# A two-dimensional Fourier filter with a gated layer: the first stage issued in one written order, and matmul banks kept in two sets

## The chip, the core and the metric

One Trainium2 chip, one core. The metric is the device time of one execution of the kernel in microseconds (us). The engines run their own instruction streams in order and wait for one another by semaphores: TensorE (PE, with its weight loads PEld), VectorE (DVE), ScalarE (ACT), GpSimd (POOL) and SyncE (SP, which here only issues DMAs). PE writes to PSUM, which has eight banks of 512 float32 columns in each of 128 partitions; DVE and ACT read it from there.

## The reference

```python
S, D, F = 2048, 640, 1728
def A(x, w_r, w_i):                       # spectral filter
    X = rfft2(x, axes=(S, D)) * (w_r + 1j * w_i)      # S x 321
    return irfft2(X, s=(S, D))
def B(x, w_gate, w_up, w_down):           # bilinear gated layer
    return ((x @ w_gate) * (x @ w_up)) @ w_down
h  = x + A(layernorm(x), w_r, w_i)
h2 = h + B(layernorm(h), w_gate, w_up, w_down)
```

Everything is float32. Where precision is to be had from the faster matmul format, operands are split into a high part in that format (fp32r) and the remainder ("lo").

## The kernel before, in words

The 2048 rows are cut into 16 tiles of 128 rows (tile t holds rows t, t+16, ...), the 321 frequencies of the row direction into parts of at most 161. Transforms are matmuls with tables.

1. **First stage** (lines 118 to 296), a loop over the 16 tiles. Each tile needs the mean and the inverse root of the variance of its rows. For 7 tiles DVE takes them (`bn_stats` L134 and L135, `bn_aggr` L136), for 9 tiles ACT does with two passes that add up (L149, L150); tiles are treated in groups of 1, 1, 2, 2, 4, 4 and 2, and each group ends in a square root on ACT (L159) and four small DVE instructions (L160 to L163). Then the row is folded onto itself: `odd` (L183, the differences, on GpSimd), `even` (L193, the sums, on DVE), and from these the 66 columns L197 and the 320 columns L198, both on DVE. The 128 x 128 table `cct` is scaled by the inverse root (L217 on DVE, L215 on ACT for tile 0). PE multiplies the folds by that table: seven products for a tile (L209, L210), each in two instructions, in two PSUM banks `im` and `re`. ACT copies them to the array `s1` with two instructions (L223, 128 columns; L228, 512 columns). Fold buffers are a ring of `NR = 4`, scaled tables a ring of four, PSUM buffers a ring of two. What the loop calls when sets the order on each engine; work on the statistics of later groups is dealt out over the tiles by `spread` and `zipped`.
2. **Filter stage**, a loop over 16 groups of columns g: `d_mm(g)` (transform of rows, banks `re`, `im`), `d_out` (ACT, L330 to L333), `s2_mm` (second transform, into one of two two-bank buffers `u` and `v` handed out by `twin`), `filt` (DVE multiplies by the complex weights, L354 to L357), `is2_mm` (inverse second transform, L389 to L398), `is2_out` (ACT and DVE copy it to `qm` and, split in high and low part, to `qr`; GpSimd corrects one row, L421 and L422). The tables of a group come by `load_wm` and `load_wi` on the SP queue, each with a ring of three. The last groups (lines 462 to 483) are written out one by one.
3. **Inverse transform of rows**, a loop over the 16 tiles: `id_mm(t)` needs all of `qm` and `qr` for the tile, `unfold` (ACT L519, DVE L523 to L525, GpSimd L527) unfolds it, `is1_mm` and `acc` add the result to x.
4. **Gated layer**, from about 175 us to the end, with weights split and combined on the way.

The order of all instructions is the order in which the program issues them (`manual_schedule`); waits follow from the data and from buffers that are used again. PSUM is handed out in pools: until the filter stage ends, one pool "a" holds `re`, `im` (two buffers each), `u` and `v`. It is closed at line 645, and the inverse transform opens "py" (`y`, two pairs of banks) and "pthree" (`eo`, two pairs). A tile of a new pool waits for what last used those banks.

Of the kernel before, what the change touches and what calls it, by code (L numbers as in the profile page):

```python
# [24 lines left out]
NR = 4  # L25
ON_ACT = (1, 4, 10, 14)
EPS = 1e-5
# [19 lines left out]
def tile_spectral_glu(ctx: ExitStack, tc: tile.TileContext, x, wf, wgu, wlast, wdown, wdlast,  # L47
# [12 lines left out]
    def banks(key, name):  # L60
        if key in pools:
            open_pools[key].close()
        open_pools[key] = ExitStack()
        pools[key] = open_pools[key].enter_context(tc.tile_pool(name=name, bufs=2, space=bass.MemoryType.PSUM))

    def bank(tag, bufs=2):
        return pools["a"].tile([P, 512], F32, tag=tag, name=tag, bufs=bufs)

    def pair(tag):
        return pools["a" if tag == "eo" else "y"].tile([P, 2, 512], F32, tag=tag, name=tag, bufs=2)  # L70
# [41 lines left out]
    fold = home("qm", [P, NR * 1026 + 2 * D], "fold")  # L112
# [3 lines left out]
    crs, edge = ([cut(bits, 1536 + 512 * h + P * i, P) for i in range(4)] for h in range(2))  # L116
# [7 lines left out]
    def moments(ts, junk=None, total=None):  # L124
        n = len(ts)
        m2 = small.tile([P, n], F32, tag="m2", name="m2")
        ve = small.tile([P, n], F32, tag="ve", name="ve")
        if junk is None:
            mv = small.tile([P, n, 2], F32, tag="mv", name="mv")

            def one(t, i):
                st = small.tile([P, 2, 6], F32, tag="st", name="st")
                return [
                    lambda: nc.vector.bn_stats(st[:, 0], X[t][:, 0:320]),  # L134
                    lambda: nc.vector.bn_stats(st[:, 1], X[t][:, 320:640]),  # L135
                    lambda: nc.vector.bn_aggr(mv[:, i], st),  # L136
                ]
# [5 lines left out]
        sq = small.tile([P, n], F32, tag="sq", name="sq")  # L143
# [11 lines left out]
    def inverse_root(ve, r, n):  # L155
        sd = small.tile([P, n], F32, tag="sd", name="sd")
        w = small.tile([P, n], F32, tag="w", name="w")
# [8 lines left out]
    SC = {}  # L166

    def front(ts):
        n = len(ts)
        r = small.tile([P, n], F32, tag="r", name="r")  # L170
        junk = [fold[:, o:o + D] for o in (NR * 1026, NR * 1026 + D)]
        m2, ve, fs = moments(ts, junk * 2 if ts[0] in ON_ACT else None)
        for i, t in enumerate(ts):
            SC[t] = r[:, i:i + 1], m2[:, i:i + 1]
        return fs, inverse_root(ve, r, n)

    def folded(t):
        o = t % NR * 1026
        return fold[:, o:o + 642], fold[:, o + 642:o + 1026]

    def odd(t):
        f = folded(t)[0]
        nc.gpsimd.tensor_tensor(view(f, 0, [[160, 2], [1, 160]]), view(XP[t], 1, [[320, 2], [1, 160]]),  # L183
                                view(XP[t], 639, [[-320, 2], [-1, 160]]), op=OP.subtract)

    def even(t):
        f, j = folded(t)

        def both(n):
            return view(f, 0, [[320, 2], [1, n]]), view(f, 160, [[321, 2], [1, n]])  # L190

        return [
            lambda: nc.vector.scalar_tensor_tensor(view(f, 320, [[161, 2], [1, 161]]),  # L193
                                                   view(XP[t], 0, [[320, 2], [1, 161]]), SC[t][1],
                                                   view(XP[t], 640, [[-320, 2], [-1, 161]]),
                                                   op0=OP.subtract, op1=OP.add),
            lambda: tt(view(j, 33, [[-33, 2], [1, 33]]), *both(33), op=OP.add),  # L197
            lambda: tt(view(j, 64, [[1, 2], [2, 160]]), *both(160), op=OP.subtract),  # L198
        ]

    PS1, CR = {}, {}

    def s1_mm(t):
        pm, pr = PS1[t] = bank("im"), bank("re")
        (f, j), c = folded(t), CR[t]
        sums = [(f[:, o:o + P], f[:, o + n:o + n + P]) for o, n in ((31, 160), (353, 161))]
        for k, ls in enumerate((*sums, (view(j, 128, [[2, P]]),), (view(j, 129, [[2, P]]),))):
            for n, l in enumerate(ls):
                nc.tensor.matmul(pm[:, k * P:(k + 1) * P], l, c, start=n == 0, stop=n == len(ls) - 1)  # L209
        nc.tensor.matmul(pr[:, 0:P], j[:, 0:P], c, start=True, stop=True)  # L210

    def scale_c(t):
        CR[t] = crs[t % 4]
        if t == 0:
            act(CR[t], cct, AF.Copy, scale=SC[t][0])  # L215
        else:
            nc.vector.tensor_scalar(CR[t], cct, SC[t][0], None, op0=OP.mult)  # L217

    def at(base, t):
        return view(base, 4 * t, [[64, 32], [1, 4]])  # L220

    def s1_rest(t):
        act(at(s1[:, 4], t), PS1[t][1][:, 0:P].rearrange("p (g m) -> p g m", g=32), AF.Copy)  # L223

    def s1_main(t):
        n = 4 if t < NT - 1 else 2
        for c in range(0, 4, n):
            act(view(s1, 4 * t + 2048 * c, [[2048, n], [64, 32], [1, 4]]),  # L228
                PS1[t][0][:, c * P:(c + n) * P].rearrange("p (c g m) -> p c g m", c=n, g=32), AF.Copy)
# [5 lines left out]
    banks("a", "pone")  # L235
    dve = [[] for _ in range(NT)]
# [1099 lines left out]
```

## Time and profile before

| | |
|---|---|
| median of 3 runs | 703.7 us (703.69 to 704.72) |
| the profiled execution | 704.37 us, its span 702.6 us |
| PE busy | 686.4 us (98%) |
| weight loads | 605.2 us (86%) |
| DVE | 478.9 us (68%) |
| GpSimd | 375.6 us (53%) |
| ACT | 305.0 us (43%) |
| DMA | 60.30 MB, mean 86 GB/s |

A row of a timeline gives the start in us from the beginning of the span, the length in us, the engine, the line, the operation, the tile written and the tiles read, their shapes, how many instructions are merged in the row, and in brackets how long the engine had stood idle before it and what released it. A row of a group gives the count, the total busy time in us and the mean of one in ns. A row of a stage gives the busy time of each engine with its instruction count and then the granted PE clock as a share of full speed. Durations overlap a little on DVE and ACT (an instruction starts before the last has quite ended), so costs in a full stream are read from one start to the next.

### The profile page before, as it was taken

What the parts mean: (1) busy time and instruction counts of PE and PEld (TensorE: products, weight loads), DVE (VectorE), ACT (ScalarE), POOL (GpSimd) and SP (SyncE); (2) the same over time, 40 slices, a digit from 0 to 9 for tenths busy, and PEclk for the clock granted to TensorE, in tenths of its full rate; (3) what the DMA queues carried; (4) which work ended last, traced back from release to release, by engine and by line L of the source; (5) the groups of instructions that cost most, each with busy time, mean ns of one, the idle gap of its engine ahead of it and who ended that gap; (6) DMA issues with size and microseconds to landing.
All of it is one profiled execution on the core that took longest, in us unless ns stands there. A gap on an engine that the chain in (4) does not pass through costs nothing.

```text
span 702.6 us, 10125 instructions
## 1 busy us (share of the span) xinstructions
PE 686.4 (98%) x3784; PEld 605.2 (86%) x3784; DVE 478.9 (68%) x832; ACT 305.0 (43%) x584; POOL 375.6 (53%) x355
## 2 busy tenths in 40 slices
PE   7899998999999999999999999999999999999998
PEld 7789997987888898988888889888888988888887
DVE  7968887699888445656565658664666656565654
ACT  4866776356543323242523356252333342424320
POOL 3312225332154586877868643158596977868610
PEclk9999999999999999999999999999999999999999
DMA  9406764002321211203020263311211102030203
GB/s 335 185 6 204 227 210 166 1 0 94 132 76 38 75 39 37 76 1 113 0 86 28 94 219 118 113 38 37 76 38 58 55 11 102 0 107 7 75 1 150
DMA packets 23233, 60.30 MB, mean 86 GB/s; under 512 B 2576, under 2 KB 7184, under 8 KB 23184
## 3 DMA queue, kind: packets, MB, share of 16 engines
q1 hardware_dynamic: 22608, 57.94, 24.0%
q0 software_dynamic: 288, 1.48, 0.6%
q8 instruction: 30, 0.49, 0.3%
q10 hardware_dynamic: 288, 0.23, 0.1%
q14 instruction: 19, 0.16, 0.1%
HBM read 51.78 MB, written 7.86 MB: 85 GB/s over the span
## 4 chain that ended last, share of the span: by engine, by line
PE 87%; DVE 8%; ACT 3%; issue 2%; DMA 1%; DVEq 0%
PE e L82 47%; PE y L82 26%; PE re L82 2%; PE im L82 2%; PE eo L82 2%; PE v L342 1%; PE im L209 1%; DVE ex L777 1%; PE u L342 1%; PE e L570 1%; DVE x L540 1%; ACT fold L149 1%; DMA x<-in_x_dram 1%; ACT fold L150 1%; DVE q L523 1%
## 5 line engine op out<-in xcount | busy, mean ns | idle before, releaser
L82 PE MATMUL e<-xt,wst 128*128 128x512 f32 x864 | 219.1, 391 | 0.0
L82 PEld LDWEIGHTS e<-xt,wst 128*128 128x128 f32 x864 | 157.9, 188 | 27.3 <-DVE m L1037 0.3
L82 PE MATMUL y<-wd,ht 128*128 128x320 f32 x880 | 150.6, 309 | 0.1
L82 PEld LDWEIGHTS y<-wd,ht 128*128 128x128 f32 x880 | 138.9, 188 | 11.3 <-DVE xb L538 0.6
L741 POOL TENSOR_TENSOR wst<-raw,wst 128x1024 fp32r<-128x1024 f32 x24 | 59.6, 2485 | 90.7 <-ACT wst L740 78.4
L82 PE MATMUL e<-t,wst 128*128 128x512 f32 x288 | 74.2, 391 | 0.0
L757 POOL TENSOR_TENSOR wst<-raw,wst 128x896 fp32r<-128x896 f32 (+1 forms) x46 | 65.1, 1438 | 7.8 <-ACT wst L752 7.8
L952 DVE TENSOR_TENSOR xb<-y,xb 128x640 f32<-128x640 f32 x60 | 49.4, 824 | 26.4 <-PE y L82 24.5
L773 ACT ACTIVATE ht<-e 128x512 fp32r<-128x512 f32 x48 | 27.6, 596 | 86.1 <-DVE rawh L870 44.2
L82 PEld LDWEIGHTS e<-t,wst 128*128 128x128 f32 x288 | 52.6, 188 | 8.6
L952 DVE TENSOR_TENSOR x<-y,x 128x640 f32<-128x640 f32 x48 | 39.5, 823 | 21.1 <-PE y L82 19.6
L1037 DVE TENSOR_TENSOR m<-e,m 128x512 f32<-128x512 f32 x24 | 16.5, 687 | 46.1 <-ACT m L1030 28.6
L777 DVE TENSOR_TENSOR ht<-e,ht 128x512 fp32r<-128x512 f32 x48 | 33.0, 688 | 16.8 <-ACT ht L773 16.3
L752 ACT ACTIVATE wst<-raw 128x896 fp32r<-128x896 f32 (+1 forms) x48 | 30.1, 677 | 31.1 <-POOL raw L746 30.4
L82 PE MATMUL y<-ex,ht 128*128 128x320 f32 x216 | 43.5, 310 | 0.0
L82 PE MATMUL e<-xt,wdir 128*128 128x512 f32 x180 | 42.1, 392 | 0.0
L494 POOL TENSOR_TENSOR wd<-draw,wd 128x640 fp32r<-128x640 f32 x10 | 15.6, 1576 | 46.2 <-ACT wd L493 46.2
L82 PEld LDWEIGHTS e<-xt,wdir 128*128 128x128 f32 x180 | 33.5, 188 | 7.2 <-issue 0.2
L82 PEld LDWEIGHTS y<-ex,ht 128*128 128x128 f32 x216 | 36.3, 188 | 3.1
L908 ACT ACTIVATE wd<-draw 128x640 fp32r<-128x640 f32 x18 | 13.3, 740 | 58.7 <-POOL draw L921 48.1
L82 PE MATMUL e<-ht,wst 128*128 128x512 f32 x144 | 38.4, 392 | 0.0
L538 DVE TENSOR_TENSOR x<-y,x 128x640 f32<-128x640 f32 x32 | 26.2, 819 | 15.9 <-PE y L82 15.9
(228 smaller groups left out, 1300.5 us busy)
## 6 DMA issues: line engine op xcount, KB each, us to landing
raw<-in_wgu_dram SPq DMA_DIRECT2D x24, 640.0 KB, 4.0
wts<-in_wf_dram SPq DMA_DIRECT2D x16, 644.0 KB, 4.4
draw<-in_wdown_dram SPq DMA_DIRECT2D x24, 320.0 KB, 4.5
x<-in_x_dram SPq DMA_DIRECT2D x16, 320.5 KB, 6.1
bits<-in_mm_dram SPq DMA_DIRECT2D x32, 128.0 KB, 4.0
sp<-x SPq DMA_DIRECT2D x8, 320.0 KB, 2.2
xb<-sp SPq DMA_DIRECT2D x8, 320.0 KB, 6.1
out_dram<-x SPq DMA_DIRECT2D x8, 320.0 KB, 2.2
```

What stands on the lines that cost most here:

```text
L82: nc.tensor.matmul(o, l, r, start=start, stop=stop, skip_group_check=True)
L342: nc.tensor.matmul(ps[h][:, 0:NQ], WM[g][0][:, h], T[g][:, h], start=True, stop=True)
L494: los.append(lambda r=r, a=a, b=b: engine.tensor_tensor(w[:, 1, a:b], r, f32(w[:, 0, a:b]), op=OP.subtract))
L538: tt(xv, ps[:, :, 0:320], xv, op=OP.add)
L741: nc.gpsimd.tensor_tensor(wa[:, 1], stage[:, 0:1024], f32(wa[:, 0]), op=OP.subtract)
L752: act(ws[:, 0, o:o + b - a], stage[:, a:b], AF.Copy)
L757: ptt(ws[:, 1, o:o + b - a], stage[:, a:b], f32(ws[:, 0, o:o + b - a]), op=OP.subtract)
L773: act(unit(u)[0], src, AF.Copy)
L777: engine.tensor_tensor(lo, src, f32(hi), op=OP.subtract)
L908: act(w[:, 0, a:b], r, AF.Copy)
L952: tt(xv, PQ[q][:, :, 0:320], xv, op=OP.add)
L1037: tt(m5, acc_a, m5, op=OP.add)
```

## The change

In the first stage:

- The loop is replaced by a list of steps, `ORDER`, which is the order of issue for all engines. Its letters: b, c, a = `bn_stats` twice and `bn_aggr`; i, q = the two passes of ACT; m, v = the small steps behind the statistics; r = the square root; n = the four steps of the inverse root; t = a scaled table; o, s, k, d = the fold's four parts (odd, even, 66 columns, 320 columns); X, Y, Z, W = the products of a tile; p = the copy; h = a one-element copy on GpSimd that reads another step's result, and so makes GpSimd wait for that step.
- The odd fold stays on GpSimd for tiles 0 to 6, behind such holds, and goes to DVE for tiles 7 to 15.
- Scaled tables: ACT makes those of tiles 0, 6 to 9, 10 to 13 and 14 to 15 (one instruction for each); DVE that of tile 1, and those of tiles 2 and 3, and 4 and 5, as one instruction for each pair. All 16 tables have a place of their own.
- The products of a tile go to one two-bank PSUM buffer, of which four are in turn (two `f`, and `u` and `v`), and one ACT instruction copies its 640 columns (the last tile's: three).
- The fold ring has 6 places in place of 4.

In the crossing to the inverse transform:

- PSUM is held in two sets: pool "y" (first `f`, then `re` and `im`, then `y`) and pool "a" with `u` and `v` alone, which stays open from the first stage until the gated layer.
- `id_mm` is split in `id_main` (the products from `qm`) and `id_rest` (from `qr`) and writes to `u` and `v`. Tiles 0 and 1 issue both main parts before both rests.
- The last groups are issued in another order: group 10's copies come behind `s2_mm` of groups 14 and 15, between the parts of group 14's filter; group 13's product goes to `re`, `im` and group 14's to a two-bank buffer; copies are moved between ACT and DVE, and the tables of groups 14 and 15 are loaded behind the products of groups 11 and 12.

The diff, cut to its core:

```diff
-NR = 4
+NR = 6
+GROUPS = ((0,), (1,), (2, 3), (4, 5), (6, 7, 8, 9), (10, 11, 12, 13), (14, 15))
 ON_ACT = (1, 4, 10, 14)
+ON_POOL = (0, 1, 2, 3, 4, 5, 6)
+TABLES_ON_ACT = (0, 6, 10, 14)
+ORDER = """
+b0 o0 c0 i1 a0 m0 v0 s0 q1 b2 h.s0 o1 frt c2 r0 a2 v1 n0.0 s1 r1 i4 n1.0 n0.1 d0 n0.2 n1.1 k1 i5 n1.2 n0.3 b3 h.k1
+o2 c3 t0.0 q5 a3 X0 m2 v2 n1.3 s2 Y0 r2 t1 q4 Z0 n2.0 d2 X1 n2.1 d1 Y1 v3 n2.2 b6 r3 Z1 n3.0 n2.3 k0 W1 t2 i10 W0
+n3.1 k2 X2 s3 Y2 b8 h.d1 o3 q10 Z2 b7 n3.2 W2 d3 p1 X3 n3.3 k3 s4 Y3 p0 c6 h.s3 o4 Z3 i12 c7 W3 t3 b9 q12 X4 h.s4 o6
+c9 Y4 c8 p3 h.s3 o5 a8 a7 a6 i14 a9 X5 v4 d4 i11 k4 Z4 s5 W4 d5 r4 Y5 p2 n4.0 k5 Z5 n4.1 p4 n4.2 W5 n4.3 m4 o7 t4.7
...
+i15 X11 o14 Y11 o12 q15 Z11 s12 W11 k12 X12 d12 Y12 v6 o13 r6 p9 Z12 n6.0 s13 W12 p10 X13 d13 Y13 k13 p11 n6.1 n6.2
+Z13 n6.3 s14 t6.14 W13 t6.15 X14 k14 d14 p12 Y14 o15 p13 Z14 s15 W14 X15 k15 d15 p14 Y15 Z15 W15 p15
+"""
...
+        def odd():
+            (nc.gpsimd if t in ON_POOL else nc.vector).tensor_tensor(
+                view(f, 0, [[160, 2], [1, 160]]), view(x0, 1, [[320, 2], [1, 160]]),
+                view(x0, 639, [[-320, 2], [-1, 160]]), op=OP.subtract)
...
+    def s1_copy(t):
+        ps = PS1[t].rearrange("p a b -> p (a b)")
+        for c, e in ((0, 5),) if t != LAST else ((0, 2), (2, 4), (4, 5)):
+            act(view(s1, 4 * t + 2048 * c, [[2048, e - c], [64, 32], [1, 4]]),
+                ps[:, c * P:e * P].rearrange("p (c g m) -> p c g m", c=e - c, g=32), AF.Copy)
...
+        if ts[0] in TABLES_ON_ACT:
+            for i, t in enumerate(ts):
+                steps[f"t{g}.{t}"] = lambda t=t, s=r[:, i:i + 1]: act(CR[t], cct, AF.Copy, scale=s)
+        elif n == 1:
+            steps[f"t{g}"] = lambda t=ts[0], s=r: nc.vector.tensor_scalar(CR[t], cct, s, None, op0=OP.mult)
         else:
+            o = crs[:, ts[0] * P:(ts[0] + n) * P].rearrange("p (t m) -> p t m", t=n)
+            steps[f"t{g}"] = lambda o=o, r=r, n=n: tt(o, view(cct, 0, [[0, n], [1, P]]), view(r, 0, [[1, n], [0, P]]),
+                                                      op=OP.mult)
...
+    for k in order:
+        if k[0] == "h":
+            f, j = folded(int(k[3:]))
+            done = dict(o=f[:, 0:1], s=f[:, 320:321], k=j[:, 0:1], d=j[:, 383:384])[k[2]]
+            nc.gpsimd.tensor_copy(small.tile([P, 1], F32, tag="hold", name="hold"), done)
         else:
+            steps[k]()
...
+    banks("y", "ptwo")
...
     s2_mm(NG - 2)
     s2_mm(NG - 1)
+    early = filt_half(NG - 2, 0, True)
+    main, high, low = outs[NG - 6]
+    early[0]()
+    main()
+    high()
+    early[1]()
+    low()
+    early[2]()
+    early[3]()
+    load_wi(NG - 3)
+    product(NG - 5, 1 - turn[0])
+    product(NG - 4, turn[0])
     load_wi(NG - 2)
+    load_wi(NG - 1)
+    second, third, fourth = filt_half(NG - 2, 1), filt_half(NG - 1, 0), filt_half(NG - 1, 1)
+    outs[NG - 5][1]()
     second[0]()
     second[1]()
+    product(NG - 3)
+    outs[NG - 5][0](nc.vector)
+    third[0]()
+    third[1]()
+    outs[NG - 5][2]()
+    product(NG - 2, 1 - turn[0])
+    outs[NG - 4][1]()
+    outs[NG - 4][0]()
+    fourth[0]()
+    fourth[1]()
+    product(NG - 1)
+    outs[NG - 4][2]()
+    outs[NG - 3][1]()
+    outs[NG - 3][0](nc.vector)
+    outs[NG - 2][1]()
+    outs[NG - 2][0]()
+    outs[NG - 1][0]()
+    outs[NG - 3][2]()
+    outs[NG - 2][2]()
+    outs[NG - 1][1](nc.vector)
+    outs[NG - 1][2]()
...
+    def id_main(t):
+        ps = PE_[t] = twin((t + turn[0]) % 2)
...
-    open_pools.pop("a").close()
-    del pools["a"]
     banks("y", "py")
-    banks("a", "pthree")
...
-    id_mm(0)
-    id_mm(1)
+    id_main(0)
+    id_main(1)
+    id_rest(0)
+    id_rest(1)
     unfold(0, [])
     id_mm(2)
```

(`outs[g]` holds the three parts of `is2_out(g)`: [0] the copy to `qm`, [1] the high part and the odd row, [2] the low part with GpSimd's correction; `product(g)` issues `is2_mm(g)`.)

More of the change, by code (lines that the diff above doesn't have):

```diff
@@ L142, in moments @@
             return m2, ve, fs
-        sq = small.tile([P, n], F32, tag="sq", name="sq")
+        sq = tiny("sq", n)
         fs = []
@@ L212, in scale_c @@
[L212 to L229, printed above, removed]
+    SC, CR = {}, {}
@@ L454, in tile_spectral_glu @@
         d_out(g + 2)
-        if back is not None:
-            is2_out(back)
+        if back is not None and g + 3 < NG:
+            main, high, low = is2_out(back)
+            high()
+            low()
+            main()
             load_wi(back + 3)
```

279 lines of the change are left out of this document (124 added, 155 removed).

## The prediction

> **What bounds the kernel now.** I read the busy shares by stage first, then the waits of each stage that the change touches, and then single instructions in order of time.
>
> ```profile
> span 702.6 us, 10125 instructions
> 0.00:45.70 45.70, 38.19 (x272) 34.79 (x272) 37.46 (x123) 28.54 (x77) 15.67 (x23) 1.00 0.54 200
> 45.70:110.20 64.50, 64.50 (x418) 59.14 (x419) 51.36 (x70) 45.06 (x114) 13.89 (x34) 1.00 0.62 196
> 110.20:126.70 16.50, 13.21 (x90) 12.29 (x89) 10.10 (x22) 8.27 (x20) 8.96 (x18) 0.90 0.29 101
> 126.70:175.00 48.30, 47.12 (x276) 40.30 (x275) 44.16 (x105) 26.22 (x54) 15.37 (x16) 1.00 0.09 35
> 122.00:126.00 4.00, 4.00 (x19) 4.00 (x19) 1.19 (x3) 0.44 (x1) 0.84 (x4) 0.57 0.00 0
> ```
>
> Columns: stage, length, busy time of PE, weight loads, DVE, ACT, POOL, granted clock, DMA share, GB/s. The filter stage (45.7 to 110.2) keeps PE busy all the time, and nothing in it is edited: it only moves. PE is short of work in the first stage and in the crossing to the inverse transform (110.2 to 126.7), where it stands still for 3.3 us and then runs at a lowered clock. In the last row the clock is 0.57 over 4 us, so 4 x 0.43 = 1.7 us are lost to it. Everything behind 175 us is four fifths of the span and is not touched.
>
> The first stage belongs to DVE. Its first and last instructions, and one late tile with GpSimd's fold beside it and one without:
>
> ```profile
> 4.83 0.49 DVE L134 BATCH_NORM_STATS2 st<-x 128x6 f32<-128x320 f32 x1 [3.83 <-DMA x<-in_x_dram]
> 4.88 0.86 POOL L183 TENSOR_TENSOR fold<-x 128x320 f32<-128x320 f32 x1 [4.43 <-DMA x<-in_x_dram]
> 35.51 0.55 DVE L193 SCALAR_TENSOR_TENSOR fold<-x,m 128x322 f32<-128x322 f32 x1
> 35.63 1.15 POOL L183 TENSOR_TENSOR fold<-x 128x320 f32<-128x320 f32 x1 [1.64 <-DVE bits L217]
> 36.16 0.70 DVE L197 TENSOR_TENSOR fold<-fold 128x66 f32<-128x66 f32 x1
> 36.90 0.49 DVE L198 TENSOR_TENSOR fold<-fold 128x320 f32<-128x320 f32 x1
> 37.31 0.28 DVE L217 TENSOR_SCALAR bits<-cct,r 128x128 f32<-128x128 f32 x1
> 37.50 0.55 DVE L193 SCALAR_TENSOR_TENSOR fold<-x,m 128x322 f32<-128x322 f32 x1
> 42.95 0.55 DVE L193 SCALAR_TENSOR_TENSOR fold<-x,m 128x322 f32<-128x322 f32 x1
> 43.60 0.23 DVE L197 TENSOR_TENSOR fold<-fold 128x66 f32<-128x66 f32 x1
> 43.87 0.49 DVE L198 TENSOR_TENSOR fold<-fold 128x320 f32<-128x320 f32 x1
> L193 DVE SCALAR_TENSOR_TENSOR fold<-x,m 128x322 f32<-128x322 f32 x16 | 9.3, 578 | 0.0
> L197 DVE TENSOR_TENSOR fold<-fold 128x66 f32<-128x66 f32 x16 | 6.3, 393 | 0.9
> L217 DVE TENSOR_SCALAR bits<-cct,r 128x128 f32<-128x128 f32 x15 | 5.5, 367 | 0.4
> ```
>
> DVE works from 4.83 to 44.36 (43.87 + 0.49), 39.5 us, with hardly a gap. The tile beginning at 35.51 takes 1.99 us to the next tile's L193. The 66-column sum L197 lasts 0.70 us where GpSimd folds at the same time (35.63 to 36.78) and 0.23 where it doesn't (43.60), and GpSimd's fold is stretched to 1.15 from 0.86. So the two engines take turns, and a fold on GpSimd beside DVE's sums costs DVE almost as much as doing it itself. Beside the statistics (4.83 and 4.88) the statistics stay at 0.49.
>
> **The change, first stage.** I work by difference on those 39.5 us.
> - Taking turns goes. Excess of the group means over the undisturbed rows: L197 16 x (0.393 - 0.23) = 2.6; L217 15 x (0.367 - 0.28) = 1.3; L193 16 x (0.578 - 0.55) = 0.45. Together 4.4 us. Seven folds stay on GpSimd, held back until DVE is at statistics; they cost between nothing (the row at 4.83) and 7/16 of 4.4 = 1.9. I take nothing, since the holds put each of them beside statistics.
> - Nine folds come to DVE: each reads two inputs over 320 columns, as L198 does, whose start to the next start is 0.41 (36.90 to 37.31): +3.7.
> - Tables: one of 15 on DVE cost 0.19 from its start to the next (37.31 to 37.50), 2.9 in all. DVE keeps one single table (0.19) and two for pairs of tiles, 256 columns wide, between L217's 0.19 and L198's 0.41; I take 0.36, as nearer to the latter in columns. Net -2.0.
> - The sums, statistics and inverse roots are as many as before, in another order: no change from their number. What hides their waits is the interleaving; where an inverse root waits for ACT's square root behind a 0.8 us square, DVE stands. Walking the order by hand I meet one such place, 0.2 us, near 11.8; I allow 0 to 1 and take none beyond what the old order had.
>
> Sum: -4.4 + 3.7 - 2.0 = -2.7. DVE then ends near 41.6. Its bounds are -3.5 (cheaper table pairs, waits of the old order gone) and 0 (1.9 of turns kept, 1 us of waits).
>
> Does something else take over? ACT and PE:
>
> ```profile
> 6.35 0.72 ACT L149 ACTIVATE fold<-x 128x640 f32<-128x640 f32 x1
> L228 ACT ACTIVATE s<-im 128x512 f32<-128x512 f32 x15 | 8.8, 583 | 0.0
> L150 ACT ACTIVATE fold<-x,m 128x640 f32<-128x640 f32 x9 | 7.4, 827 | 0.2
> L149 ACT ACTIVATE fold<-x 128x640 f32<-128x640 f32 x9 | 6.6, 729 | 0.0
> L215 ACT ACTIVATE bits<-cct,r 128x128 f32<-128x128 f32 x1 | 0.4, 385 | 0.0
> L580 ACT ACTIVATE xt<-y 128x640 fp32r<-128x640 f32 x5 | 3.5, 704 | 3.1 <-PE y L570 3.1
> 8.96 1.53 PE L209 MATMUL im<-bits,fold 128*128 128x128 f32 x12
> 43.70 1.53 PE L209 MATMUL im<-bits,fold 128*128 128x128 f32 x12
> 45.07 0.39 PE L210 MATMUL re<-bits,fold 128*128 128x128 f32 x2
> 17.03 0.75 PE L209 MATMUL im<-bits,fold 128*128 128x128 f32 x4 [1.12 <-DVE fold L198]
> ```
>
> ACT gets ten more tables (0.385 each, eleven in all: 4.2) and one copy of 640 columns for each tile in place of two. The copy reads two PSUM banks; L580 does the same in 0.704. Its work: 9 x (0.827 + 0.729) = 14.0 of statistics, 4.2, 16 x 0.704 = 11.3: 29.5 us from 6.35, where it starts on the second tile now, so about 35.9 plus its waits. That is some 5.7 us ahead of DVE's end: not the bound, and the added tables hide behind DVE. PE does 12 of a tile's 14 matmuls in 1.37 (43.70 to 45.07), 0.114 each, 1.6 a tile, 25.6 in all. Its first real matmul needs the first table, which the order puts behind another tile's square on ACT: near 10.9 instead of 8.96; 10.9 + 25.6 = 36.5, still 5 us ahead. Today the warming matmuls run up to the first real one; the new pause of 1.9 us between them therefore costs nothing by itself. Memsets, holds and GpSimd's DMA issue lie on GpSimd, which has 30 us to spare. The SP queue is not reordered here. The tail behind DVE's last sum stays: last matmuls, the copy in three pieces where it was two and one.
>
> **The change, crossing.**
>
> ```profile
> 110.97 0.41 PEld L389 LDWEIGHTS u<-bits,ring 128*65 128x65 f32 x4 [0.52 <-ACT qm L419]
> 114.54 0.41 PEld L389 LDWEIGHTS u<-bits,ring 128*65 128x65 f32 x4 [0.89 <-ACT qm L419]
> 118.37 0.39 PE L398 MATMUL re<-bits,y 128*128 128x128 f32 x2
> 118.91 0.69 DVE L416 COPY qm<-re 128x512 f32<-128x512 f32 x1
> 120.81 0.42 DVE L417 TENSOR_TENSOR qr<-im,qr 64x256 fp32r<-64x256 f32 x1 [0.44 <-ACT qr L412]
> 121.33 1.60 PE L82 MATMUL eo<-tab,qm 128*128 128x161 f32 x8 [2.58 <-issue]
> 121.65 0.45 POOL L422 TENSOR_TENSOR qr<-bits,qr 1x128 fp32r<-1x128 f32 x1
> 124.31 0.44 ACT L519 ACTIVATE s<-eo 128x322 f32<-128x322 f32 x1 [3.53 <-PE eo L82]
> 125.19 0.48 DVE L524 TENSOR_TENSOR q<-eo,s 128x322 f32<-128x322 f32 x1
> 126.70 1.26 PE L82 MATMUL eo<-tab,qm 128*128 128x161 f32 x8
> ```
>
> PE's last second-transform matmul ends at 118.76. The inverse transform starts at 121.33, right behind DVE's last split (120.81 + 0.42 = 121.23), although the main table qm is complete at 119.60 (118.91 + 0.69). What it waits for is the bank pool, closed and opened over the banks that DVE reads. The change leaves that pool open and puts the tiles into the two-bank buffers of the filter stage.
> - Products end sooner: group 13's product waited 0.89 us for ACT to empty its buffer (114.54). It moves to the single banks, free by then. Group 11's waited 0.52 (110.97); group 10's copies, moved ahead on ACT, end that some 0.3 sooner. PE ends near 117.6 instead of 118.76, -1.2. What isn't seen is how the last groups' inverse tables land: each can be loaded only when the product three groups earlier has freed its buffer, so the gain lies between 0 and 1.4; I take 1.2, since these products move earlier too.
> - The last copy to qm moves to ACT at once behind it: near 118.1 instead of 119.60. PE starts there, -3.2 against 121.33.
> - Main products of two tiles run first (16 matmuls at about 0.14, a row of 8 being 1.26 with the end of the last: 2.2 us, to 120.4). They cover GpSimd's last correction (before 121.65 + 0.45 = 122.1, now about 119.7). Without that cover the rest would wait 0.4.
> - PE no longer stands 2.6 us, only about 0.5, so the 1.7 us of lowered clock go.
> - Given back: tile 2 needs the first buffer, which the unfolding frees 1.36 us after ACT begins (124.31 to 125.67). In the new order that is near 122.75 while PE is done at 121.9, a new wait of 0.85.
>
> Tile 2 then starts at 122.75 instead of 126.70: -3.9. From there PE (47.1 of 48.3 us) and DVE (44.2) do what they did, so this stays. Bounds: -2.2 (the clock falls anyway) to -4.3 (tables no wait, copies earlier).
>
> Total -2.7 - 3.9 = -6.6 against the profiled execution's 704.37 (span 702.6 and 1.8 around it): 697.8. The median of the runs is 703.7, 0.67 lower; I carry the difference over and say **697.1**.
>
> The clock: the Trainium skill, "TensorE: Matmul & The Clock Gate", section "What's actually happening", says that the array falls to half clock after an idle window of about 3.4 us that runs freely. The 1.7 us lost here are 3.4 us at half clock, which agrees; the gap before it was only 2.58 us, which by that rule need not have sufficed. By it the removal of the gap would be worth nothing in executions where the window falls otherwise.
>
> **Rivals.**
> - The clock regains nothing: the median executions never lost it, or the two small new pauses lower it again. For it: 17.03 shows a 1.12 us pause without loss, 121.33 one of 2.58 with; the new pauses (0.5, 0.85) are below both, but the median is below the profiled time. Time 697.1 + 1.7 = 698.8.
> - The written order gains nothing in the first stage: every engine waits in line, DVE loses at roots and turns what it saves. For it: 2.7 us over the 119 instructions that the order gives DVE are 23 ns each. Time 703.7 - 3.9 = 699.8. That the crossing gives nothing, its table loads landing late, would be 703.7 - 2.7 = 701.0.
> - Slower: PE falls to half clock in the first stage, in its longer pauses (1.9 us behind the warming matmuls, which lies between the two rows; by my walk some 1.5 us twice around tile 4, ahead of which the order puts the statistics of tiles 6 to 9). PE has 5 us to spare and the sum 6.6, so it decides only from 11.6 us lost, 23 us at half clock. Through the whole stage: 10.9 + 2 x 25.6 = 62 against 45.5, +16.6 - 3.9, 716.4. Against it: one fall costs 1.7 us, less than the spare time.
>
> **Chances.** Forecast 0.60, clock 0.12, no first-stage gain 0.13, no crossing gain 0.05, slower 0.05; 0.05 for both gains eaten by waits (no change). Own range of the forecast: 695 to 699. The range for 8 in 10 runs from 694.6 (both lower bounds, -3.5 and -4.3, with some of the 0.67) to 700.4 (past the two middle rivals). A measurement here can tell about 0.2%, 1.4 us, from no change: faster 0.90, same 0.05, slower 0.05.
>
> **What would show it.** DVE's last sum of the first stage near 41.6 and L197's counterpart at 0.23 throughout; folds on DVE 0.41 apart; ACT's 640-column copy near 0.70; the first inverse-transform matmul 3.3 us sooner behind the filter stage's end than now, with the clock at 1.00 and a wait of about 0.85 before tile 2; the stages behind unchanged in length. I am wrong if DVE shows idle time behind ACT's roots, if GpSimd's seven folds still lengthen DVE's sums, or if the late products wait for their tables.

## The result: 699.0 us against 703.7, and where it came from

The changed kernel takes 698.98 us (median of 4 runs, 698.82 to 699.43) against 703.7 of the kernel before on the same chip (703.25 to 704.72). The ratio over the runs on record is 0.9926, its 95% interval 0.9914 to 0.9938 (the two medians alone would give 0.9933). The profiled execution took 699.12 us, its span 697.3 us. The forecast was 697.1, inside a range of 694.6 to 700.4, so time and sign came out as forecast. The working behind them did not: two terms were off by about 2 us and more each, in opposite directions, and a third, of 2 us, was missing.

The stages of the changed kernel, cut at the events that cut those of before (span, then columns: stage, length, busy time of PE, weight loads, DVE, ACT, POOL, granted clock, DMA share, GB/s):

```profile
span 697.3 us, 10083 instructions
0.00:40.33 40.33, 35.25 (x272) 33.87 (x272) 32.65 (x120) 30.60 (x73) 7.66 (x19) 1.00 0.61 227
40.33:104.83 64.50, 64.50 (x418) 59.13 (x419) 51.84 (x71) 45.54 (x115) 13.94 (x34) 1.00 0.61 196
104.83:119.25 14.42, 11.72 (x89) 10.56 (x88) 9.78 (x21) 7.94 (x21) 8.09 (x18) 1.00 0.34 113
119.25:167.55 48.30, 47.16 (x273) 40.37 (x274) 44.45 (x106) 25.83 (x53) 16.25 (x16) 1.00 0.09 35
```

The first stage is 5.37 us shorter (40.33 against 45.70). The filter stage only moved. The crossing, up to tile 2 of the inverse transform, is 14.42 us where it was 16.50, and its clock is 1.00 where it was 0.90. That makes -7.45 at tile 2; the span is only 5.3 us shorter, so 2.1 us were lost again behind it.

For the experiments I read five starts in each trace and give the stretches between them, in us: the filter stage's first matmul; from there to the first inverse matmul (a); from there to the first output tile, PE's first `y<-yt,tab` (b); from PE's first `e<-xt,wst` to its first `y<-wd,ht`, the entry of the gated layer (c); and from there to the end (d). What lies between b and c is 66.61 to 66.67 in every kernel. The last columns are the span, the median time and the ratio to runs of the kernel before on the same chip. The medians of before were 703.73 for `repeat` to `addr`, 704.08 for `early_free` to `folds_pool`, 704.30 for the last four.

| kernel | filter starts | a | b | c | d | span | time | ratio (95%) |
|---|---|---|---|---|---|---|---|---|
| before | 45.70 | 75.63 | 9.05 | 6.83 | 498.75 | 702.6 | 703.7 | |
| changed | 40.33 | 74.16 | 8.53 | 7.30 | 500.32 | 697.3 | 698.98 | 0.9926 (0.9914 to 0.9938) |
| repeat | 40.38 | 74.28 | 8.53 | 7.11 | 500.36 | 697.3 | 698.84 | 0.9937 (0.9924 to 0.9951) |
| cross_only | 45.91 | 74.12 | 8.51 | 6.81 | 498.70 | 700.7 | 702.33 | 0.9985 (0.9976 to 0.9994) |
| k_alone | 44.89 | 75.64 | 7.44 | 6.82 | 498.85 | 700.3 | 703.19 | 0.9994 (0.9984 to 1.0003) |
| addr | 40.53 | 74.15 | 8.50 | 7.27 | 498.61 | 695.7 | 697.60 | 0.9920 (0.9907 to 0.9934) |
| early_free | 40.23 | 73.11 | 8.95 | 7.28 | 500.47 | 696.7 | 698.31 | 0.9918 (0.9904 to 0.9931) |
| fill | 45.65 | 75.61 | 7.45 | 6.81 | 498.63 | 700.8 | 703.12 | 0.9991 (0.9982 to 1.0) |
| pools_only | 45.56 | 74.16 | 8.68 | 6.87 | 498.48 | 700.4 | 702.46 | 0.9981 (0.9972 to 0.999) |
| folds_pool | 42.80 | 74.15 | 8.52 | 6.94 | 500.23 | 699.3 | 701.33 | 0.9959 (0.9946 to 0.9971) |
| best | 40.46 | 73.27 | 8.94 | 6.90 | 498.81 | 695.0 | 696.91 | 0.9901 (0.9887 to 0.9914) |
| pad | 40.31 | 74.28 | 8.51 | 6.83 | 498.76 | 695.3 | 697.35 | 0.9909 (0.9895 to 0.9922) |
| moved | 45.61 | 75.65 | 7.46 | 6.90 | 500.24 | 702.5 | 705.75 | 1.0021 (1.0011 to 1.003) |
| fill11 | 45.66 | 75.66 | 7.44 | 7.30 | 498.91 | 701.6 | 703.24 | 0.9989 (0.998 to 0.9997) |

One plain warning for column b: the 9.05 of the kernel before holds 1.6 us of lowered clock, which not every execution has; `k_alone` and `moved`, whose code there is the same, and `fill` and `fill11`, the same but for the fillers, show 7.44 to 7.46 without it.

**First stage.** Timeline of DVE near the end of the stage:

```profile
37.04 0.48 DVE L203 TENSOR_TENSOR fold<-x 128x320 f32<-128x320 f32 x1
37.44 0.55 DVE L208 SCALAR_TENSOR_TENSOR fold<-x,crs 128x322 f32<-128x322 f32 x1
38.09 0.23 DVE L229 TENSOR_TENSOR fold<-fold 128x66 f32<-128x66 f32 x1
38.24 0.48 DVE L231 TENSOR_TENSOR fold<-fold 128x320 f32<-128x320 f32 x1
```

Timeline of GpSimd's first and third fold, and of PE's first products:

```profile
4.80 0.87 POOL L203 TENSOR_TENSOR fold<-x 128x320 f32<-128x320 f32 x1 [3.96 <-DMA x<-in_x_dram]
9.36 0.85 POOL L203 TENSOR_TENSOR fold<-x 128x320 f32<-128x320 f32 x1
10.18 3.73 PE L214 MATMUL f<-crs,fold 128*128 128x128 f32 x28 [1.26 <-ACT crs L276]
```

Groups of the first stage (count, then busy us and the mean in ns):

```profile
L208 DVE SCALAR_TENSOR_TENSOR fold<-x,crs 128x322 f32<-128x322 f32 x16 | 8.8, 548 | 0.1
L229 DVE TENSOR_TENSOR fold<-fold 128x66 f32<-128x66 f32 x16 | 3.6, 222 | 0.8
L281 DVE TENSOR_TENSOR crs<-cct,crs 128x256 f32<-128x256 f32 x2 | 1.1, 560 | 0.0
L239 ACT ACTIVATE s<-f 128x640 f32<-128x640 f32 x8 | 5.3, 691 | 0.4 <-PE f L214 0.4
```

DVE ends at 38.24 + 0.48 = 38.72 instead of 44.36. The 66-column sum L229 (L197 before) is 0.222 in the mean where it was 0.393: no fold stands against it any more. GpSimd's folds take 0.75 to 0.87 beside the statistics, folds on DVE stand 0.40 apart, ACT's 640 columns take 0.691, and PE's first product starts at 10.18 behind a pause of 1.26 us (10.9 and 1.9 in the forecast). All this is about as forecast. What is not: the 320-column sum starts 0.15 us behind the 66-column sum (38.09, 38.24), where it was 0.27 (43.60, 43.87).

**Crossing.** The timeline where PE waits, and the rows of GpSimd and DVE that explain it:

```profile
106.79 2.78 POOL L368 TENSOR_TENSOR us<-us,wts 128x322 f32<-128x322 f32 x3
107.70 1.14 DVE L361 TENSOR_TENSOR y<-y,us 128x322 f32<-128x322 f32 x1 [0.89 <-POOL us L368]
108.76 0.68 DVE L409 COPY qm<-u 128x512 f32<-128x512 f32 x1
110.45 0.42 DVE L419 TENSOR_TENSOR qr<-u,qr 64x256 fp32r<-64x256 f32 x1
111.13 0.62 PE L385 MATMUL u<-bits,y 128*65 128x128 f32 x4 [1.38 <-DVE qr L419]
113.38 0.60 PE L385 MATMUL im<-bits,y 128*65 128x128 f32 x4
114.49 1.36 PE L98 MATMUL v<-tab,qm 128*128 128x161 f32 x8 [0.52 <-ACT qm L407]
119.25 1.34 PE L98 MATMUL v<-tab,qm 128*128 128x161 f32 x8 [0.81 <-DVE q L562]
```

The first inverse matmul starts 74.16 us behind the filter stage's start instead of 75.63. The two small pauses 0.52 and 0.81 are those forecast, but there is one of 1.38 that was not. DVE's joining of group 14's filter (107.70) stands 0.89 us and then takes 1.14 instead of 0.49 beside three multiplications of GpSimd; the copies that empty `u` (108.76 and 110.45) are queued behind it, so the product of group 14, which needs `u`, waits.

### The profile page after: what moved, and what is told of

Its sections match the earlier page's. It is cut to its first block, busy times and chain, and to the rows that moved or that the text cites. A ratio compares the mean times of both kernels' runs of the same rounds, so it can differ in the third digit from the quotient of the medians.

```text
span 697.3 us, 10083 instructions
## 1 busy us (share of the span) xinstructions
PE 684.0 (98%) x3784; PEld 602.8 (86%) x3784; DVE 473.8 (68%) x829; ACT 306.8 (44%) x580; POOL 368.3 (53%) x351
## 4 chain that ended last, share of the span: by engine, by line
PE 84%; DVE 11%; issue 2%; DMA 1%; ACT 1%; POOL 0%; SPq 0%; DVEq 0%; ACTq 0%; POOLq 0%
PE e L98 45%; PE y L98 26%; PE re L98 2%; PE im L98 2%; PE v L342 1%; PE v L98 1%; DVE ex L814 1%; PE u L342 1%; PE f L214 1%; PE u L98 1%; DVE x L578 1%; DMA raw<-in_wgu_dram 1%; DVE q L561 1%; PE u L385 1%; DVE q L562 1%
```

## The experiments

**repeat.** The changed kernel itself, once more.

> The changed kernel as it is, for a second profile. The first one put the start of the filter stage 5.4 us earlier than before, tile 2 of the inverse transform 7.4 us earlier, and the end only 5.3 us earlier: 2.0 us were given back in the gated layer, 0.7 at its entry and 1.3 in small steps of about 0.1 us for each column of it. Theory: both losses belong to the program, and the second profile shows them again within 0.3 us; time 698.8 to 699.4. Rival: they belong to that one execution; then the shift at the end is near 7.3 us in this profile, 697 us.

698.84 us (698.58 to 699.12): the same kernel in another series, and every stretch but c within 0.12 us.

**cross_only.** The first stage of before (its loop, four fold places, copies of 128 and 512 columns) ahead of the changed crossing:

```diff
-NR = 6
+NR = 4
...
-            steps[k]()
...
+        s1_mm(t)
+    s1_main(NT - 1)
+    s1_rest(NT - 1)
```

> The kernel before with the crossing's part of the change alone (bank pools in two sets, the last groups in the new order, main products of two tiles first); the first stage is the old loop. Theory (the parts add up): the crossing is worth 2.1 us up to tile 2 of the inverse transform, as the first profile of the changed kernel has it, and the start of the filter stage stays at 45.7: 701.6 without any loss behind, up to 702.3 with the 0.7 us at the entry. Rival (the prediction as written): 3.9 us, 699.8, because the late product does not wait when the first stage is old.

702.33 us. The crossing alone is worth 1.4 us at the median, and it has the same waits as in the changed kernel, so they don't come from the first stage:

```profile
116.67 0.62 PE L391 MATMUL u<-bits,y 128*65 128x128 f32 x4 [1.38 <-DVE qr L425]
120.03 1.37 PE L82 MATMUL v<-tab,qm 128*128 128x161 f32 x8 [0.52 <-ACT qm L413]
```

From the filter's start to the first output tile (a + b) it has 82.63 us, the kernel before 84.68 with its lowered clock and `k_alone` 83.08 without. The crossing's gain is thus 2.0 us where the clock fell and 0.45 where it didn't. To the end, 3.4 us of span lie between `cross_only` and the changed kernel: 5.6 of the first stage less what was lost behind.

**k_alone.** The kernel before, with the 66 columns laid out so that they don't share two columns with the 320 columns that DVE writes next:

```diff
-    o = t % NR * 1026
-    return fold[:, o:o + 642], fold[:, o + 642:o + 1026]
+    o = t % NR * 1030 + 2
+    return fold[:, o:o + 642], fold[:, o + 644:o + 1028]
```

> The kernel before with one thing from the change: the 66 columns of the fold are written in an order that no longer overlaps the 320 columns written by the next instruction (two of 386 columns were written by both). Theory: the next instruction waited for that write; start to start 0.27 becomes 0.15 us, 16 x 0.12 = 1.9 us of the first stage, time 701.8; this is the term missing in the prediction. Rival: GpSimd's turns take the place of the wait, the stage keeps its length: 703.7 (0 to 0.5 us gained).

703.19 us, which alone can't be told from no change, where 701.8 was expected; but the trace shows the effect. Timeline of DVE, a pair of the kernel before with a fold beside it, then of `k_alone` a pair with a fold and one without:

```profile
38.16 0.58 DVE L197 TENSOR_TENSOR fold<-fold 128x66 f32<-128x66 f32 x1
38.77 0.49 DVE L198 TENSOR_TENSOR fold<-fold 128x320 f32<-128x320 f32 x1
```

```profile
37.64 0.58 DVE L197 TENSOR_TENSOR fold<-fold 128x66 f32<-128x66 f32 x1
38.14 0.48 DVE L199 TENSOR_TENSOR fold<-fold 128x320 f32<-128x320 f32 x1
42.79 0.23 DVE L197 TENSOR_TENSOR fold<-fold 128x66 f32<-128x66 f32 x1
42.93 0.48 DVE L199 TENSOR_TENSOR fold<-fold 128x320 f32<-128x320 f32 x1
```

Without a fold beside it, the pair is 0.14 apart instead of 0.27; with one, 0.50 instead of 0.61. So a wait of some 0.12 us goes in both cases, and GpSimd's turns don't take its place. The expected 1.9 us counted sixteen pairs, but in the kernel before only nine have the 320 columns directly behind the 66; in the other seven another instruction stands between. That makes 9 x 0.12 = 1.1 us. From start to the next start the 66 columns take 0.97 us less in all (5.08 against 6.04), and the filter starts 0.8 us sooner. In the changed kernel eight pairs stand directly behind one another, and these are 0.14 to 0.15 apart.

**folds_pool.** The changed kernel with the nine folds back on GpSimd:

```diff
-ON_POOL = (0, 1, 2, 3, 4, 5, 6)
+ON_POOL = tuple(range(16))
```

> The changed kernel with all sixteen first folds on GpSimd, each beside the statistics, instead of seven there and nine on DVE. Theory as predicted (a fold beside the statistics costs DVE nothing; nine on DVE cost 3.7 us): DVE ends the first stage up to 3.7 us sooner if ACT and the waits let it, time between 695.5 and 698. Rival (the folds come too late or stand against DVE's sums: GpSimd's fold is as long as DVE's statistics of a tile, and DVE waits): the first stage is as long as now or longer, 699 to 701, with waits of DVE for GpSimd's folds or 66-column sums of 0.5 us and more.

701.33 us, the rival: 2.4 us slower than the changed kernel, the filter starting at 42.80. Timeline of GpSimd and DVE, then DVE's group of the 66 columns:

```profile
18.53 2.60 POOL L203 TENSOR_TENSOR fold<-x 128x320 f32<-128x320 f32 x3
20.44 0.78 DVE L229 TENSOR_TENSOR fold<-fold 128x66 f32<-128x66 f32 x1
```

```profile
L229 DVE TENSOR_TENSOR fold<-fold 128x66 f32<-128x66 f32 x16 | 4.8, 299 | 1.0
```

The folds of the later tiles have no statistics to stand beside (DVE has those of seven tiles only), they run against the sums, and the 66 columns take 0.78 again. The price of 3.7 us for nine folds on DVE was right as a price, and moving them still gains: DVE's chain grows by 1.6 us when they go back (40.31 against 38.72), and the stretch from its end to the filter's start by 0.9 (2.49 against 1.61). This holds for the order as it stands, which has no holds for these nine; an order written for sixteen folds on GpSimd was not tried. The Trainium skill ("SBUF — State Buffer", section "SBUF: two separate sides") says that a DVE instruction with two SBUF inputs and a GpSimd instruction that reads SBUF exclude each other for a whole instruction; rows 18.53 and 20.44 agree, and so does 107.70 in the crossing.

**pools_only.** The kernel before, with nothing but the PSUM pools in two sets and the inverse tiles in `u` and `v`:

```diff
-        ps = PE_[t] = pair("eo")
+        ps = PE_[t] = twin((t + turn[0]) % 2)
...
-    open_pools.pop("a").close()
```

> The kernel before, with one part of the change: the PSUM pools stand in two sets, so that the inverse transform's tiles go to the two-bank buffers of the filter stage and no pool is closed between them. Order of groups, copies and first stage are as before. Theory (the pool's closing held the first inverse matmul until DVE's last split): the first inverse matmul starts at the main table's copy, some 1.6 us sooner behind the filter stage's start (near 74.0 instead of 75.63), but tile 2 only some 0.3 us sooner, since GpSimd's last correction still ends where it did; clock 1.00; time near 702.4. Rival (the pool is the whole of the crossing's gain): 701.5 or lower. Other rival (the pool held nothing): 703.7.

702.46 us, as the theory had it. Timeline of PE, and GpSimd's last correction:

```profile
119.72 1.34 PE L82 MATMUL v<-tab,qm 128*128 128x161 f32 x8 [0.96 <-ACT qm L412]
122.17 0.86 PE L82 MATMUL v<-xt,qr 128*128 128x322 f32 x4 [0.45 <-POOL qr L423]
122.87 1.26 PE L82 MATMUL u<-tab,qm 128*128 128x161 f32 x8
121.67 0.45 POOL L423 TENSOR_TENSOR qr<-bits,qr 1x128 fp32r<-1x128 f32 x1
```

With the pool open, PE starts 1.47 us sooner behind the filter's start (a = 74.16, the changed kernel's own 74.16) and then waits 0.45 for GpSimd. a + b is 82.84 against 82.69 of the changed kernel: the new order of the last groups, the moved copies and the two main parts ahead add 0.15 us to what the pools alone bring.

**early_free.** The changed kernel with group 11's outputs, which empty `u`, issued ahead of the second half of group 14's filter:

```diff
+    outs[NG - 5][0](nc.vector)
+    outs[NG - 5][2]()
     second[1]()
-    outs[NG - 5][0](nc.vector)
     product(NG - 3)
...
-    outs[NG - 5][2]()
```

> The changed kernel, with the last groups' outputs reordered so that the buffer of the products is emptied before DVE and GpSimd go on with the third part of the group behind it. Nothing else differs. In the changed kernel the product of group 14 waited 1.38 us for that buffer. Theory (PE's wait there sets the start of the inverse transform): the wait goes or falls below 0.3 us, the first inverse matmul comes 1.0 to 1.4 us sooner behind the filter stage's start (near 72.9 instead of 74.2 us) and the time is near 697.7 against 698.9 of the changed kernel. Rival (DVE's and GpSimd's own chain of corrections ends where it ended, and main products only wait elsewhere): the product starts sooner but the second tile of the inverse starts where it did, 698.9.

698.31 us: between the two. Timeline of PE:

```profile
109.98 0.62 PE L385 MATMUL u<-bits,y 128*65 128x128 f32 x4 [0.35 <-ACT qr L412]
113.34 1.36 PE L98 MATMUL v<-tab,qm 128*128 128x161 f32 x8 [0.32 <-ACT qm L407]
116.11 0.86 PE L98 MATMUL v<-xt,qr 128*128 128x322 f32 x4 [0.16 <-POOL qr L422]
118.52 1.34 PE L98 MATMUL v<-tab,qm 128*128 128x161 f32 x8 [0.81 <-DVE q L562]
```

The wait is 0.35 instead of 1.38 and the inverse starts 1.05 us sooner behind the filter's start, but GpSimd's corrections now come last (116.11), and the output tile gains 0.63 (a + b 82.06 against 82.69). So the 1.38 us were a real loss, worth about 0.6.

**fill and fill11.** The kernel before with eight, then eleven matmuls that compute nothing read, in the 2.6 us in which PE stood still:

```diff
+    idle = twin(turn[0])
+    for n in range(FILL):                     # 8, then 11
+        nc.tensor.matmul(idle[:, 0, 0:P], cct, cct, start=True, stop=True)
```

> The kernel before, with eight matmuls of 128 columns on a used-up buffer put behind the filter stage's last product, so that PE works some 1.8 us of the 2.6 us in which it stood still ahead of the inverse transform. They compute nothing that is read. Theory (the standing still lowers the clock in some executions of the kernel before, by 1.7 us of time, and that makes its times spread by 2.2 us): the clock is 1.00 there, the times lie within 0.6 us of each other, and the median falls to between 702.4 and 703.0 against 703.7. Rival (the spread has another cause): the same median and the same spread, 703.7.

> The kernel before, with eleven filling matmuls in place of eight behind the last product, some 2.7 us, so that PE hardly stands still ahead of the inverse transform (in fill 0.79 us were left, and its times still spread over 1.9 us). Theory (what is left of the pause lowers the clock in some executions): no pause above 0.2 us there, clock 1.00, times within 0.7 us of each other, median 702.5 to 702.9. Rival (the spread of the kernel before comes from elsewhere): times still spread over 1.5 us and more, median 703.0 to 703.4, which leaves the clock a part of one execution that the median may or may not hold.

703.12 us (702.53 to 704.47) and 703.24 us (702.61 to 703.78). The medians lie just past the expected 703.0 and 702.9, the second in the range of its rival (703.0 to 703.4), and the spreads of 1.9 and 1.2 us miss the expected 0.6 and 0.7. PE's timeline of `fill11`, then, of `fill`, the stretch of four microseconds that had a clock of 0.57 before, then PE's row of `moved`, whose pause is that of the kernel before:

```profile
118.57 2.62 PE L485 MATMUL v<-cct 128*128 128x128 f32 x22
121.32 1.34 PE L83 MATMUL eo<-tab,qm 128*128 128x161 f32 x8
```

```profile
122.00:126.00 4.00, 4.00 (x31) 4.00 (x30) 1.63 (x4) 0.88 (x2) 1.58 (x4) 1.00 0.00 0
```

```profile
121.26 1.34 PE L82 MATMUL eo<-tab,qm 128*128 128x161 f32 x8 [2.58 <-issue]
```

The inverse starts where it started, and b is 7.44 instead of 9.05: 1.6 us, the 1.7 of the prediction. But the pause alone doesn't bring the loss: `k_alone` and `moved` have the same pause of 2.58 us, and in their profiled executions the clock stays at 1.00 there and b is 7.44 and 7.46. So one of three profiled executions with the pause lost the 1.6 us. That agrees with the free-running window of the Trainium skill ("TensorE: Matmul & The Clock Gate", section "What's actually happening"), though by its 3.4 us a pause of 2.6 should not suffice.

How often the other executions lose it is argued, not shown. The median fell by 1.0 and 1.1 us with the fillers, the mean by 0.6 and 0.9: what a loss of 1.6 in some half of the executions would give. In the last series the 23 runs of the kernel before fall in two groups, nine at 702.61 to 703.64 and fourteen at 704.22 to 705.30, and with eleven fillers all twelve lie at 702.61 to 703.78. But of the two series of 21 runs ahead of it three and six runs lie in that gap, and with eight fillers two of eleven runs lie above 704; why was not profiled. The mean clock of an execution doesn't tell either, because the clock can also fall in the first stage, where PE has time to spare: in `cross_only` and `moved` it was 0.67 and 0.62 from 16 to 20 us, behind a pause of 1.12 us that the kernel before has too (17.03), there with 1.00.

**addr, pad and moved.** These look for the 1.6 us lost at the end (d: 498.75 before, 500.32 changed). The changed first stage asks for the buffer `spare` ahead of `qr`, so `qr` (later `t12`, the split operand of the gated layer's matmuls) begins at byte 195488 of each partition instead of 185184, and `spare` at 185184 instead of 201568. `addr` asks for `qr` first again. `pad` leaves the new sequence and shifts `qr` by 192 bytes, all behind it by 256. `moved` gives the kernel before the new sequence.

```diff
+    home("qr", [P, 2, NT, P], "qr0", F32R)          # addr, ahead of spare
-    room = [home("spare", [P, 2576], "crs")]        # pad: wider
+    room = [home("spare", [P, 2624], "crs")]
+    home("spare", [P, 2576], "spare0")              # moved, ahead of qr
```

> The changed kernel with one line more: two SBUF buffers (qr, later the split operand of the gated layer, and the small ring) are placed where the kernel before had them. In the gated layer some matmuls stood 0.2305 us apart instead of 0.2267, those that read the moved operand and some beside them, together 1.3 us. Theory: the place of the buffer makes that; with the old places the gated layer loses 0 to 0.3 us instead of 1.3 and the time falls by 1.0 to 1.3 us to about 697.8. Rival: the place does nothing, 699.0.

> The changed kernel with the buffer qr (later t12) moved by 192 bytes of each partition and all buffers behind it by 256, so that qr begins at 96 bytes past a multiple of 256, as it did in the kernel before, but in the new region behind the spare buffer, which stays where the change put it. Theory A (the alignment of qr decides): the stretch from the first down-projection to the end falls to 498.6, time 697.4. Theory B (the region, or the spare buffer's place, decides): it stays at 500.3, time 698.9.

> The kernel before, with nothing altered but that the spare buffer is placed ahead of qr, as the changed kernel places it (one line). Theory (the order of these two buffers in SBUF costs 1.7 us in the gated layers, whatever the program ahead of them): the stretch from the first down-projection to the end grows from 498.75 to 500.4, time 705.4 against 703.7. Rival (the loss belongs to the changed kernel's timing): no change, 703.7.

697.60, 697.35 and 705.75 us. In `addr` and `pad` d is back at 498.61 and 498.76; in `moved` it rises to 500.24, in a kernel whose program is otherwise that of before. PE's groups between 205 and 690 us, first of the changed kernel, then of `pad`:

```profile
L98 PE MATMUL e<-xt,wst 128*128 128x512 f32 x839 | 213.3, 392 | 0.0
L98 PE MATMUL e<-t,wst 128*128 128x512 f32 x276 | 71.8, 393 | 0.0
L98 PE MATMUL e<-ht,wst 128*128 128x512 f32 x138 | 37.2, 394 | 0.0
```

```profile
L98 PE MATMUL e<-xt,wst 128*128 128x512 f32 x837 | 212.6, 392 | 0.0
L98 PE MATMUL e<-t,wst 128*128 128x512 f32 x276 | 71.2, 391 | 0.0
L98 PE MATMUL e<-ht,wst 128*128 128x512 f32 x138 | 36.9, 392 | 0.0
```

In the two groups whose counts agree the 512-column matmuls are longer by 0.6 and 0.3 us in all, 2 ns each, with no wait in front; in the largest the counts differ by two records that the trace has or has not, and its 0.7 can't be split so finely. Nine kernels here have `qr` at the old start or, as `pad`, at the same distance from a multiple of 256 bytes (96), and their d is 498.48 to 498.91; five have 160, and theirs is 500.23 to 500.47. The region is not the cause, since `pad` stays in it and leaves `spare` where the change put it. Which access suffers, and whether 128 or 256 bytes is the period, is open.

**best.** The changed kernel with the one line of `addr` and the order of `early_free`.

> The changed kernel with both mends: the buffer qr given its old place in SBUF (one line, as in addr) and the buffer of the products emptied earlier (as in early_free). If the two gains stand in different stages and add up: 698.9 - 1.25 - 0.6 = 697.0, with the stretch from the first down-projection to the end at 498.6 and the start of the first output tile 0.6 us earlier than in addr. Rival (the gated layer takes back what the crossing gains, for its weights are loaded at their own time): 697.6, as addr.

696.91 us (696.28 to 697.28), ratio 0.9901 (0.9887 to 0.9914), the fastest of all: both mends hold, and they add up (697.0 expected). Its d is 498.81 and its a 73.27.

## Point by point: where the prediction was right and where wrong

**First stage: forecast -2.7, measured -5.4.** I added up, for each kind of DVE instruction, the time from its start to the next start, in both traces (us):

| kind | before | after | difference | forecast |
|---|---|---|---|---|
| 66 columns | 6.04 | 2.24 | -3.80 | -2.6, turns |
| even folds (322) | 9.74 | 9.14 | -0.60 | -0.45, turns |
| 320 columns | 6.90 | 6.53 | -0.37 | 0 |
| tables | 4.26 | 1.17 | -3.09 | -1.3 turns, -2.0 |
| odd folds on DVE | 0 | 3.80 | +3.80 | +3.7 |
| inverse roots, small steps | 5.74 | 3.97 | -1.77 | 0 |
| statistics | 6.85 | 7.11 | +0.26 | 0 |

These make -5.57, against 5.64 between the two ends of DVE. The tables and the nine folds were right within 0.3 us each, and so were the turns: of the 3.80 of the 66 columns 2.7 are turns (in the kernel before six of the sixteen last 0.58 to 0.76 instead of 0.23), and with the even folds that makes 3.3, where 3.05 stood. Two things were not in the sum. The step "no change from their number" failed: the inverse roots and the small steps are as many, but most now have a sum of another tile between them and the next and don't wait for the one before: 1.8 us, of which some 0.15 are turns (one step lasted 0.82 beside a fold before, at 15.07; two last 0.44 and 0.37 now, at 12.79 and 15.08). The timeline of DVE, before and then after, with two steps of a root in line (0.19 and 0.27 to the next start) and one between sums (0.08):

```profile
24.45 0.15 DVE L162 TENSOR_TENSOR w<-w,ve 128x4 f32<-128x4 f32 x1
24.64 0.16 DVE L163 SCALAR_TENSOR_TENSOR r<-w,r 128x4 f32<-128x4 f32 x1
24.91 0.69 DVE L217 TENSOR_SCALAR bits<-cct,r 128x128 f32<-128x128 f32 x1
```

```profile
33.78 0.48 DVE L203 TENSOR_TENSOR fold<-x 128x320 f32<-128x320 f32 x1
34.18 0.16 DVE L184 RECIPROCAL crs<-crs 128x2 f32<-128x2 f32 x1
34.26 0.54 DVE L208 SCALAR_TENSOR_TENSOR fold<-x,crs 128x322 f32<-128x322 f32 x1
```

And the part of the diff that moves the fold places from 1026 to 1030 columns I costed at nothing: the 66 columns no longer share two with the next output, and a pair comes 0.12 us closer where the two stand directly behind one another, nine times before: 1.1 of the 66 columns' 3.80. `k_alone` shows this one by itself. The first is read from the two traces only: no run changes the order of the small steps alone, and the change also put their results in another buffer. What made the 0.37 of the 320 columns was not taken apart. The bound of -3.5 for this stage came from looking at turns and tables alone. The tail behind DVE grew from 1.34 to 1.61 us. The feared ones didn't come: no wait of DVE behind ACT's roots, and the statistics stay at 0.47 to 0.49 beside GpSimd's seven folds. These cost some 0.5 us on the two small steps named, where nothing stood.

**Crossing: forecast -3.9, measured -2.1 at tile 2 in the profiled executions.** The step that failed is "PE ends near 117.6 instead of 118.76". Measured from the filter's start PE's last product ended 0.6 us later than before, not 1.2 sooner (113.98 - 40.33 against 118.76 - 45.70): the 1.38 us for `u`, and the wait of group 11's product, from which 0.3 was to come, only shrank from 0.52 to 0.45. I had freed the buffers by walking ACT's queue and had not walked DVE's, on which GpSimd's three multiplications fall. So the main start came 1.47 us sooner where 3.2 were forecast. The copy on ACT came 0.52 behind the end, as forecast; the lowered clock gave 1.6 back of the 1.7; the wait ahead of tile 2 was 0.81 against 0.85. The way from the first inverse matmul to the first output tile has become 1.07 us longer (b 8.51 in `cross_only` against 7.44): it starts ahead of the last correction, and waits for a buffer ahead of tile 2. So without a fall of the clock the crossing is worth 0.45 us, of which `pools_only` gives 0.24 (82.84 against 83.08); where the clock falls, it gives 1.8 of the 2.0.

**"The stages behind unchanged in length": wrong by 2.0.** 1.6 of it is the place of `qr`, shown in both directions by `addr` and `moved`. The other 0.5 is the entry c, 7.30 against 6.83. It is not the change alone: the same code gives 7.11 in `repeat`, 6.94 in `folds_pool` and 6.83 in `pad`, and `fill11`, a kernel before with fillers, has 7.30. What sets it was not found.

**The sum.** In the profiled executions: -5.4 (first stage), -1.5 and -0.5 (crossing), +2.0 (behind): -5.3, where -6.6 was forecast. The result lies almost on the rival "the clock regains nothing" (698.8), and that isn't the reason: the clock did give its 1.6 us back in the profiled execution. But that rival had one thing right. Not every execution of before has the loss, so carrying the profiled execution's gain over to medians, less only the 0.67 between them, asks too much. That 698.98 lies well inside the range is in part luck: the errors of the first stage, the crossing and the stages behind, -2.7, +1.8 and +2.0 us, left 1.1 together. The rivals without gain in the first stage (699.8) or the crossing (701.0) fall by the table; that of a half clock in the first stage (716.4) by its 1.00 in the stage's row. A single fall there did come in the profiled execution of `addr`, which has the changed first stage: behind a pause of 1.91 us the clock was 0.58 from 11 to 15 us, and the filter still started at 40.53. PE's time to spare covers one fall, as the prediction argued.

## What to carry to other kernels

Look at what an edit does to addresses as well as to instructions: print where the long-lived buffers begin before and after, and compare the stages that the edit does not touch; one line was worth 1.2 us (`addr` against `repeat`) and 1.5 us (`moved` against before). Read costs from start to start, with who stands between: small dependent instructions and outputs that share a column cost a wait that no duration shows. And when a buffer is to come free, walk every engine that empties it, with what is queued ahead of that copy.

## What the runs showed of the hardware that was not expected

- The gated layer took 498.5 to 498.9 us with `qr` at 96 bytes past a multiple of 256 (nine kernels) and 500.2 to 500.5 with it at 160 (five); matmuls of one group lasted 391 and 393 ns.
- A DVE sum of 66 columns and the next, whose outputs shared two columns, started 0.27 us apart, and 0.14 to 0.15 without the shared columns; beside a fold on GpSimd 0.61 and 0.50.
- A pause of PE doesn't settle by its length alone whether the clock falls. Behind 2.58 us it fell in one of three profiled executions (1.6 us lost in `before`, none in `k_alone` and `moved`), behind 1.12 us in the first stage in `cross_only` and `moved` and not in `before`; behind the pauses of 1.38 us and less in the crossing of the changed kernel it didn't.
